# GpSimd's differences, memsets and low parts in pieces, and a later start of the first down weight sums, in a transformer block in float16 parts

## The chip, the cores and the metric

The kernel runs on one core of a Trainium2 chip. The core has four computing engines: TensorE (PE, matrix products into PSUM), VectorE (DVE), ScalarE (ACT) and GpSimd (POOL). SyncE (SP) issues most of the DMAs. Each engine works through a queue of its own in order, and the engines wait for one another by semaphores. The metric is device time in microseconds (us) of one execution. "PEld" in the profile is PE's loading of stationary operands.

## What is computed

One pre-norm transformer block on 2048 tokens of width 640: attention with 32 heads of width 20, in which a query sees the 256 positions up to its own, and a gated feed-forward with 1536 inner columns.

```python
x = A_x                                    # 1 x 2048 x 640, float32
h = x + A(layernorm(x), wqkv, wo)          # sliding window, W = 256
h2 = h + (gelu(n @ w_gate) * (n @ w_up)) @ w_down      # n = layernorm(h)
```

## The kernel before

**Numbers.** A float32 matrix is scaled by a power of two and split into two float16 parts, high (`xh`, `w5h`) and low (`xl`, `w5l`). The high part is a cast on ACT. The low part is the scaled value less the high part, made on POOL or DVE. A product is then three float16 products.

**Order.** The program is written out once, by a planner in Python (`Clock` and the loop at the end of `block_kernel`): lanes (generators) yield an engine and a condition, a modelled clock says when an engine would be free and an operand ready, and the lane that may go issues its next instruction. What is printed is one fixed queue for each engine. `Engine.cost` holds the planner's durations. A lane's condition (`when=`) sets when the planner may issue an instruction; the chip knows only the semaphore waits that follow from the data.

**The head.** `big_lane` fills constant rows of the keys' ring `kT` with memsets on POOL, as soon as q's weights have a scale. `x_cast` makes the parts of the first two blocks of x: ACT's cast `xh`, then POOL's difference `xl`. Beside it DVE makes the low parts of k's weights (`w1l`), and DVE's `qks` takes q's products out of PSUM, so that PE's next product finds a free bank. PE fills its waits there with products of an identity (`pv<-ident`), which stand in its queue.

**The feed-forward.** It runs over four chunks of 512 tokens and three groups of 512 inner columns, each in four tiles of 128. For most of them the gate and up products are made in a scheme of seven block products instead of eight (`Quad`; Strassen's scheme as Winograd wrote it). It needs sums of weight blocks (`weight_sums`: tile `ws`, four parts: POOL makes the third, DVE the first and second, POOL the fourth, two buffers) and sums of token blocks (`token_sums`, on DVE, tiles `ts` and `wst`). The sums are made for the first twelve quads, written to DRAM and read back for the later ones. In a quad PE's results in the PSUM banks `ra`, `rb` and `tp` are copied by ACT (`rr`, `gelt`, `rs`) and summed by DVE (`gel`, `rs`).

**The down product** of the last groups uses the same scheme (`down7`). Its weight sums (`seven_weights`) are four parts of the tile `ts0`: POOL makes t1 from the low parts `w10l`, DVE t2, POOL t3, DVE t4. Its token sums (`seven_tokens`) lie in the space of `w9l`. `seven_weights` may begin, in the planner, when four quads are through.

**Normalisation.** `norm_lane` normalises the next chunk's blocks two at a time beside the quads (lanes h and i): DVE's statistics, POOL's power `lyh`, `lyi`, DVE's small steps on `lyi`, DVE's scaling `wsl`, ACT's cast of it, and transposes by DMA.

All instructions carry one line in the profile, L199, that of the planner's call; groups are told apart by their tiles.

## Time and profile before

| | before |
|---|---|
| median of 3 runs | 996.2 us (995.93 to 996.38) |
| profiled execution | 996.4 us, of which the span is 994.7 |
| PE busy | 977.8 us |
| DVE busy | 787.4 us |
| ACT busy | 485.7 us |
| POOL busy | 342.0 us, 498 instructions |
| HBM read, written | 73.73 MB, 28.84 MB |

The span runs from the first to the last instruction; 1.7 us of the execution lie around it. The mean granted clock of PE is 0.996. By stages: up to some 150 us the inputs are loaded and split and attention starts; attention runs to some 560 us; from some 640 us the quads run, with the down products between them; from 800 us all down products but the last use the scheme of seven. The profile's timeline has start, duration, engine, operation and tiles, and in brackets the idle time of that engine just before, with what ended it.

### The profile page before, as it was taken

To read this page: it belongs to the slowest core of one execution; us is meant where nothing else is said; L and a number is where in the kernel's file an instruction comes from. 1 tells how busy PE (TensorE), PEld (TensorE's weight loads), DVE (VectorE), ACT (ScalarE), POOL (GpSimd) and SP (SyncE) were. 2 spreads that over 40 slices of the span, in tenths; PEclk is the share of its full clock that TensorE was granted. 3 is DMA by queue.
4 is the path that set the end of the run, shared out by engine and by line. 5 is a ranking of instruction groups with operands and counts; after the bars stand their busy time and mean duration, and the time that the engine had idled before them with its cause. 6 is when DMAs were issued, how large, how long until landed. Compare 5 with 4: busy or idle time off the path is not lost.

```text
span 994.7 us, 35811 instructions
## 1 busy us (share of the span) xinstructions
PE 977.8 (98%) x15326; PEld 747.6 (75%) x15326; DVE 787.4 (79%) x2252; ACT 485.7 (49%) x862; POOL 342.0 (34%) x498
## 2 busy tenths in 40 slices
PE   8998999999999999999999999999999999999998
PEld 7875777777877777777766754688788888888886
DVE  7878998887876767777688798877976887788784
ACT  5615657675555555555577535343323333443431
POOL 7003335463434333344346311344303223233320
PEclk9999999999999999999999999999999999999999
DMA  8667565752522433222305543324354442223211
GB/s 314 126 124 181 148 171 161 172 140 76 112 81 70 109 87 81 72 69 70 124 31 124 113 136 104 109 80 132 119 175 106 148 144 81 80 80 107 81 54 53
DMA packets 130047, 113.01 MB, mean 114 GB/s; under 512 B 85216, under 2 KB 103392, under 8 KB 129888
## 3 DMA queue, kind: packets, MB, share of 16 engines
q1 hardware_dynamic: 117792, 99.97, 36.6%
q10 hardware_dynamic: 12096, 10.75, 3.4%
q8 instruction: 120, 1.97, 0.8%
q14 instruction: 39, 0.32, 0.1%
HBM read 73.73 MB, written 28.84 MB: 103 GB/s over the span
## 4 chain that ended last, share of the span: by engine, by line
PE 86%; DVE 8%; ACT 3%; DMA 2%; issue 1%; POOL 0%; SPq 0%; ACTq 0%; DVEq 0%
PE mm L199 40%; PE rb L199 12%; PE ra L199 12%; PE pv L199 11%; PE tp L199 9%; DVE junk L199 1%; DVE ts L199 1%; DVE am L199 1%; ACT pt L199 1%; DVE ht L199 1%; DMA wst<-in_wu_dram 0%; DVE w1l L199 0%; DMA wst<-in_wd_dram 0%; DMA pt<-in_x_dram 0%; DVE xt L199 0%
## 5 line engine op out<-in xcount | busy, mean ns | idle before, releaser
L199 POOL TENSOR_SCALAR_AFFINE_SELECT pt<-pt 128x512 f32<-128x512 f32 x352 | 176.5, 517 | 270.0 <-ACT pt L199 252.6
L199 DVE CUSTOM_DVE_ANT_0 junk<-rb,band 128x320 bf16<-128x320 f32 x232 | 113.4, 489 | 36.1 <-PE rb L199 31.1
L199 ACT ACTIVATE pt<-ra,esc 128x640 f32<-128x640 f32 (+2 forms) x132 | 100.6, 769 | 78.0 <-PE ra L199 68.8
L199 ACT ACTIVATE pt<-rb,esc 128x640 f32<-128x640 f32 (+2 forms) x124 | 94.3, 768 | 81.9 <-PE rb L199 75.4
L199 DVE CUSTOM_DVE_ANT_0 junk<-ra,band 128x320 bf16<-128x320 f32 x216 | 105.7, 489 | 33.9 <-PE ra L199 28.9
L199 PE MATMUL pv<-pt,v 128*21 128x128 f32 x2880 | 103.0, 275 | 0.3 <-ACT oT L199 0.2
L199 PEld LDWEIGHTS <-ah 128*128 128x128 f16 (+1 forms) x660 | 63.5, 98 | 23.2 <-issue 1.0
L199 PEld LDWEIGHTS <-ws 128*128 128x128 f16 x720 | 70.8, 98 | 12.9 <-issue 2.6
L199 PEld LDWEIGHTS <-qT 60*64 60x64 f16 x1280 | 29.7, 104 | 62.3 <-issue 51.3
L199 PEld LDWEIGHTS pv<-pt,v 128*21 128x21 f32 x2880 | 69.2, 100 | 9.6 <-issue 1.1
L199 PEld LDWEIGHTS <-kT 62*64 62x64 f16 x2880 | 64.4, 106 | 9.3 <-issue 5.3
L199 PEld LDWEIGHTS <-gu 128*128 128x128 f16 (+1 forms) x700 | 51.7, 98 | 26.1 <-issue 0.4
L199 DVE SCALAR_TENSOR_TENSOR ht<-mm,ffk,ht 128x320 f32<-128x320 f32 x86 | 46.9, 545 | 15.4 <-PE mm L199 14.2
L199 PE MATMUL mm<-xh,w1h 128*32 128x256 f16 (+1 forms) x344 | 55.9, 273 | 1.4 <-DVE qks L199 1.4
L199 PE MATMUL mm<-xl,w1h 128*32 128x256 f16 (+1 forms) x362 | 56.0, 273 | 0.0
L199 PE MATMUL mm<-xh,w1l 128*32 128x256 f16 (+1 forms) x356 | 55.9, 273 | 0.0
L199 ACT CAST ah<-gel 128x512 f16<-128x512 f32 x48 | 29.7, 619 | 47.8 <-DVE gel L199 47.7
L199 DVE TENSOR_TENSOR al<-gel,ah 128x512 f16<-128x512 f32 x48 | 42.3, 882 | 13.1 <-ACT ah L199 12.1
L199 ACT ACTIVATE gel<-gel,ffk 128x512 f32<-128x512 f32 x36 | 26.0, 723 | 50.2 <-DVE gel L199 50.1
L199 PE MATMUL mm<-w3h,oh 128*32 128x320 f16 (+1 forms) x364 | 49.7, 299 | 0.6 <-DVE ht L199 0.6
L199 PE MATMUL mm<-w3h,ol 128*32 128x320 f16 (+1 forms) x355 | 49.6, 299 | 0.0
L199 PE MATMUL mm<-w3l,oh 128*32 128x320 f16 (+1 forms) x355 | 49.6, 299 | 0.0
(354 smaller groups left out, 2670.2 us busy)
## 6 DMA issues: line engine op xcount, KB each, us to landing
ws<-wsums SPq DMA_DIRECT2D x24, 640.0 KB
qk<-qks ACTq DMA_DIRECT2D x32, 256.0 KB
wsums<-ws SPq DMA_DIRECT2D x12, 640.0 KB
qT<-qk SPq DMA_DIRECT2D x72, 80.0 KB
kT<-qk SPq DMA_DIRECT2D x72, 80.0 KB
ht<-in_x_dram SPq DMA_DIRECT2D x16, 320.0 KB
h_dram<-ht SPq DMA_DIRECT2D x16, 320.0 KB
ht<-h_dram SPq DMA_DIRECT2D x16, 320.0 KB
```

The costliest lines, as they stand in the source:

```text
L199: r = real(*args, **kw)
```

## The change

A helper `difference` issues a subtraction on POOL as several instructions along the first free dimension. Five kinds of differences go through it: the low parts of x's first two blocks (five columns of 128 as 2, 2 and 1), the third and fourth part of the weight sums (the same cut), the first and third down weight sums (four pieces of 320), and two of the down token sums (two pieces of 256). The memsets of `kT` are cut in four. The down weight sums may begin, in the planner, after ten quads instead of four.

```diff
+    def difference(o, a, b, n):
+        for i in range(0, o.shape[1], n):
+            k = slice(i, min(i + n, o.shape[1]))
+            nc.gpsimd.tensor_tensor(o[:, k], a[:, k], b[:, k], op=ALU.subtract)
...
-                nc.gpsimd.memset(kT[64 * par + 32:64 * par + 64, :, r, :].bitcast(F32), pair)
+                for p in range(0, H // 2, 4):
+                    nc.gpsimd.memset(kT[64 * par + 32:64 * par + 64, p:p + 4, r, :].bitcast(F32),
+                                     pair)
...
-        nc.gpsimd.tensor_tensor(lo, src, hi, op=ALU.subtract)
+        difference(lo, src, hi, 2)
...
-        yield on("gpsimd", when=lambda: pos["quads"] >= FT and W["u", 1].spent
+        yield on("gpsimd", when=lambda: pos["quads"] >= 2 * FT + 2 and W["u", 1].spent
...
-            nc.gpsimd.tensor_tensor(t1, d2, d1, op=ALU.subtract)
+            difference(t1, d2, d1, 1)
...
-            nc.gpsimd.tensor_tensor(t3, t2, d1, op=ALU.subtract)
+            difference(t3, t2, d1, 1)
...
-                nc.gpsimd.tensor_tensor(s2, s1, h1, op=ALU.subtract)
+                difference(s2, s1, h1, 2)
...
-                nc.gpsimd.tensor_tensor(s3, h1, h2, op=ALU.subtract)
+                difference(s3, h1, h2, 2)
...
-        nc.gpsimd.tensor_tensor(t[:, 2], gl, ul, op=ALU.subtract)
+        difference(t[:, 2], gl, ul, 2)
...
-        nc.gpsimd.tensor_tensor(t[:, 3], gh, t[:, 1], op=ALU.subtract)
+        difference(t[:, 3], gh, t[:, 1], 2)
```

The change moves instructions. In the head, POOL's queue (`kT` the keys' ring, `xl` the low parts of the first two blocks, `lyxc` the power of the third block's normalisation) reads so, with - for before and + for the change:

```order
 L199 TENSOR_TENSOR lyxb<-lvexb,mhalf 128x1
-L199 MEMSET kT 32x16x64 x12
-L199 TENSOR_TENSOR xl<-gu,xh 128x5x128 x2
+L199 MEMSET kT 32x4x64 x40
+L199 TENSOR_TENSOR xl<-gu,xh 128x2x128 x2
+L199 TENSOR_TENSOR xl<-gu,xh 128x128
+L199 TENSOR_TENSOR xl<-gu,xh 128x2x128 x2
+L199 TENSOR_TENSOR xl<-gu,xh 128x128
 L199 TENSOR_TENSOR lyxc<-lvexc,mhalf 128x1
+L199 MEMSET kT 32x4x64 x8
```

Eight of the 48 shorter memsets now stand behind `xl` and `lyxc`.

In the quads, about 690 to 750 us, POOL's queue before reads (`ws` weight sums, `lyh` and `lyi` powers of the normalisation, `ts` the down weight sums of w10):

```order
L199 TENSOR_TENSOR ws<-w5l,w8l 128x640
L199 TENSOR_TENSOR ws<-w5h,ws 128x640
L199 TENSOR_TENSOR ts_16367<-w10l 128x1280
L199 TENSOR_TENSOR ts_16367<-ts_16367,w10l 128x1280
L199 TENSOR_TENSOR lyh<-lveh,mhalf 128x1
L199 TENSOR_TENSOR lyi<-lvei,mhalf 128x1
L199 TENSOR_TENSOR ws<-gu 128x640
```

and in the change, from the same pair of weight sums on:

```order
L199 TENSOR_TENSOR ws<-w5l,w8l 128x256 x2
L199 TENSOR_TENSOR ws<-w5l,w8l 128x128
L199 TENSOR_TENSOR ws<-w5h,ws 128x256 x2
L199 TENSOR_TENSOR ws<-w5h,ws 128x128
L199 TENSOR_TENSOR lyh<-lveh,mhalf 128x1
L199 TENSOR_TENSOR lyi<-lvei,mhalf 128x1
L199 TENSOR_TENSOR ts_16903<-w10l 128x320 x4
L199 TENSOR_TENSOR ts_16903<-ts_16903,w10l 128x320 x4
L199 TENSOR_TENSOR ws<-gu 128x256 x2
```

The sums of w10 have gone behind the next pair of powers; the first four pieces wait for no semaphore there, the second four for DVE's sum.

On DVE the two sums that belong to them go some sixty rows back. What now stands there (`rs`, `gel` the quad's sums, `ht` the down product's accumulation):

```order
L199 TENSOR_TENSOR rs<-rb,rs 128x256
L199 TENSOR_TENSOR gel<-rb,rr 128x256
L199 SCALAR_TENSOR_TENSOR ts_16903<-w10h,ts_16903 128x1280
L199 SCALAR_TENSOR_TENSOR ts_16903<-ts_16903,w10h 128x1280
L199 SCALAR_TENSOR_TENSOR ht<-mm,ffk,ht 128x320
L199 TENSOR_TENSOR rs<-ra,gelt 128x256
```

Between `gel` and `ht` there was nothing before; the two stood between accumulations of two quads earlier. PE's and SP's queues hold the same operations in the same order as before; on ACT one activation moves by two rows.

## The prediction

> **What bounds the kernel now.** I read the page's busy shares and its chain first, then the windows, to see where TensorE (PE) has room at all.

> ```profile
> PE 977.8 (98%) x15326; PEld 747.6 (75%) x15326; DVE 787.4 (79%) x2252; ACT 485.7 (49%) x862; POOL 342.0 (34%) x498
> PE 86%; DVE 8%; ACT 3%; DMA 2%; issue 1%; POOL 0%; SPq 0%; ACTq 0%; DVEq 0%
> ...
> 92.00:96.00 4.00, 2.16 (x39) 1.03 (x37) 3.83 (x10) 2.29 (x5) 2.12 (x3) 1.00 0.81 237
> 96.00:100.00 4.00, 3.71 (x31) 2.21 (x35) 3.43 (x16) 2.78 (x5) 1.40 (x1) 0.57 0.54 168
> ...
> 703.00:707.00 4.00, 1.80 (x15) 1.18 (x13) 3.96 (x4) 1.10 (x3) 2.48 (x1) 1.00 0.41 164
> 707.00:711.00 4.00, 4.00 (x22) 2.94 (x22) 4.00 (x7) 1.17 (x4) 0.28 (x1) 0.57 0.44 122
> ...
> 800.00:960.00 160.00, 160.00 (x1372) 133.99 (x1370) 130.42 (x205) 64.27 (x142) 45.34 (x27) 1.00 0.27 94
> ```

> The first two lines are the page, the others windows (from:to, length, then busy time of PE, weight loads, DVE, ACT, POOL, and the granted clock). PE is the path: it is busy 98%, and from 800 to 960 us without a break. GpSimd (POOL) has two thirds of its time free and none of the chain, so its pieces matter only where they hold up VectorE (DVE) or PE. PE's losses are few. The largest lies at 703 to 711 us: 2.20 us idle (4.00 less 1.80), and then a clock of 0.57 over 4 us, which is 0.43 x 4 = 1.72 us of lost clock. At 92 to 100 us the same pair stands: 1.84 us idle, then 0.57.

> The timeline shows who made the larger gap.

> ```profile
> 700.62 0.83 DVE L199 SCALAR_TENSOR_TENSOR ws<-ws,w8h 128x640 f16<-128x640 f16 x1 [0.31 <-POOL ws L199]
> 701.52 1.40 POOL L199 TENSOR_TENSOR ws<-w5h,ws 128x640 f16<-128x640 f16 x1 [0.94 <-DVE lyai L199]
> 701.54 1.39 DVE L199 TENSOR_TENSOR lyi<-lyi,lyai 128x1 f32<-128x1 f32 x1
> 702.41 0.71 PE L199 MATMUL ra<-ts,ws 128*128 128x256 f16 x5
> 702.88 2.60 POOL L199 TENSOR_TENSOR ts<-w10l 128x1280 f16<-128x1280 f16 x1
> 702.97 2.85 DVE L199 TENSOR_SCALAR wsl<-wsl,lmvi,lyi 128x640 f32<-128x640 f32 x1
> 705.90 0.72 ACT L199 CAST wsl<-wsl 128x640 f16<-128x640 f32 x1 [6.59 <-DVE wsl L199]
> 706.53 0.37 ACT L199 COPY rr<-tp 128x256 f32<-128x256 f32 x1
> 706.95 1.03 PE L199 MATMUL tp<-h1l,ws 128*128 128x256 f16 x5 [2.20 <-ACT rr L199]
> ...
> 779.67 1.39 POOL L199 TENSOR_TENSOR ws<-gu,ws 128x640 f16<-128x640 f16 x1 [0.94 <-DVE lyai L199]
> 781.11 0.61 DVE L199 TENSOR_SCALAR wsl<-wsl,lmvi,lyi 128x640 f32<-128x640 f32 x1
> 782.85 0.42 PEld L199 LDWEIGHTS <-ws 128*128 128x128 f16 x4 [0.16 <-issue]
> ```

> DVE's one-element `lyi` takes 1.39 us because POOL's `ws` runs; its scaling `wsl` takes 2.85 us because POOL's `ts` of 2.60 us began just ahead. ACT's cast waits for `wsl`, ACT's copy `rr` stands behind that cast, and PE behind `rr`. The last three rows are a natural control 79 us later: the same normalisation beside the same `ws`, but no `ts` behind it. There `wsl` takes 0.61 us, and PE loses 0.16.

> **The change part by part.** Prices of a piece first, by shape:

> ```profile
> L199 POOL TENSOR_TENSOR ws<-w6h,ws 128x640 f16<-128x640 f16 x4 | 5.6, 1399 | 11.4 <-DVE ws L199 11.4
> L199 POOL TENSOR_TENSOR ts<-w11l 128x1280 f16<-128x1280 f16 x2 | 5.2, 2610 | 20.1 <-PE mm L199 20.1
> L199 POOL MEMSET kT<- 32x1024 f32 x12 | 11.5, 1004 | 0.1
> L199 POOL MEMSET mask<- 128x256 f32 x1 | 0.3, 312 | 0.0
> ```

> From 640 to 1280 elements a difference grows by 1.211 us, so 1.89 ns an element and 0.19 us fixed. Estimates: 256 elements 0.67 us, 128 0.43, 320 0.79. A 640 difference becomes 1.77 instead of 1.40, a 1280 one 3.17 instead of 2.61. All pieces together add some 22 us to an engine that is idle for 650.

> (a) The moved `ts` and the gap at 703. In the order, POOL's `ts` of w10 now stands behind the next `lyh`, `lyi`, so nothing follows `ws` at 702.9. `lyi` waits for one piece of `ws` (0.67 for 1.40), then `wsl` for the next (0.67): 1.34 against 1.40, even. The quad's first `ws`, ahead of DVE's sum at 700.62, ends 0.3 later, three pieces for one, and all behind it with it. So I take the control's 0.16 plus some of the 0.3: a gap of 0.3 us is left, 1.9 us gained (0 left if `wsl` passes ahead of the second piece; 0.9 left if it waits for both).

> (b) The clock. With 0.3 us idle in place of 2.20 I expect no dip: 1.7 us gained (0, if the dip has another cause).

> (c) At 632.73 a DVE sum waits for a `ws` in the same way.

> ```profile
> 632.73 1.63 DVE L199 SCALAR_TENSOR_TENSOR ws<-w9h,w9l 128x640 f16<-128x640 f16 x1
> 634.87 0.30 PE L199 MATMUL mm<-w10h,ah 128*128 128x320 f16 x1 [0.22 <-DVE ht L199]
> ```

> A piece takes at most 0.67, so PE's 0.22 us goes: gain 0.2 (bounds 0 and 0.22). At 782.85 the later `ws` costs what it may cost in (a): loss 0.3 (bounds 0 and 0.6).

> (d) The head. POOL's memsets and `xl` stand beside DVE's low parts `w1l`, which hold up the `qks` that PE waits for.

> ```profile
> 7.45 11.58 POOL L199 MEMSET kT<- 32x1024 f32 x12
> 17.65 1.34 ACT L199 CAST xh<-gu 128x640 f16<-128x640 f32 x2
> 19.11 3.34 POOL L199 TENSOR_TENSOR xl<-gu,xh 128x640 f16<-128x640 f32 x2
> 19.76 1.43 DVE L199 SCALAR_TENSOR_TENSOR w1l<-gu,sw,w1h 128x640 f16<-128x640 f32 x1
> 21.18 1.95 DVE L199 SCALAR_TENSOR_TENSOR w1l<-gu,sw,w1h 128x640 f16<-128x640 f32 x1
> 23.46 1.66 DVE L199 SCALAR_TENSOR_TENSOR w1l<-gu,sw,w1h 128x640 f16<-128x640 f32 x2
> 25.04 0.74 DVE L199 SCALAR_TENSOR_TENSOR qks<-mm,qs,qks 128x512 f16<-128x512 f32 x1
> 25.83 0.27 PE L199 MATMUL mm<-xh,w1h 128*128 128x256 f16 x1 [1.38 <-DVE qks L199]
> ```

> A `w1l` alone takes 0.83 (1.66 for two), so the first two wait 0.60 and 1.12 us: 1.72 in all. A memset of 256 costs between 0.24 (a quarter of 11.58/12) and 0.312 (the mask's row); twelve followed each other at 0.04 less than their duration, so I take 0.27. Forty then end at 18.25 instead of 19.03, and `xl` starts when ACT's first cast is done, near 18.35, 0.76 earlier. It lasts 3.4 instead of 2.8, so 2.0 us of it is left at 19.76. If DVE waits for every piece, it waits about as long as before; where its sums follow each other without a gap, or an operation with one SBUF input comes between, it doesn't: at best 0.9 is won. I take 0.2. If memsets cost 0.312, they end at 19.93; `xl` then alternates with five `w1l` and ends near 20.6 + 3.4 + 4 x 0.83 = 27.3, and PE, which needs it at its second product, loses 1.5 (2.4, if two `w0l` get in between). Two scalings of DVE that run beside the first memsets end sooner, and I cost that at nothing: the copies behind them stand on ACT behind its sums of q's weights; without that cover it would be a gain, of less than one memset, 1.0 us.

> (e) The new place of `ts`. Its rows have no wait there, so POOL starts as soon as `lyi` is done, at 733.35 in times of before, right under the next normalisation.

> ```profile
> 709.16 1.48 DVE L199 SCALAR_TENSOR_TENSOR ts<-w10h,ts 128x1280 f16<-128x1280 f16 x1
> ...
> 732.79 0.56 POOL L199 TENSOR_TENSOR lyi<-lvei,mhalf 128x1 f32<-128x1 f32 x1
> 733.51 0.61 DVE L199 TENSOR_SCALAR wsl<-wsl,lmvh,lyh 128x640 f32<-128x640 f32 x1
> 735.28 0.42 DVE L199 TENSOR_TENSOR rs<-ra,rr 128x256 f32<-128x256 f32 x1
> 737.50 0.71 PE L199 MATMUL ra<-h1h,w6l 128*128 128x256 f16 x5
> 743.15 0.42 DVE L199 TENSOR_TENSOR rs<-ra,gelt 128x256 f32<-128x256 f32 x1
> 746.76 0.71 PE L199 MATMUL ra<-h1h,w6l 128*128 128x256 f16 x5
> ```

> Four pieces of 0.79 alternate with `wsl`, `lyi` and the second `wsl`. Two waits of 0.6 to 0.8 put `rs` 1.4 us later, to 737.1 at its end; PE needs that bank at 737.50. Then DVE's own two sums of `ts`, 1.48 each (the first row, where no POOL work lies beside it), move in ahead of 743.15: with a wait of 0.8 for a piece, `rs` ends near 746.9, and PE wants its bank at 746.76. So the margins are 0.4 and about nothing; I take a loss of 0.4 (bounds 0 and 1.5, by one more piece at each place).

> (f) The other pieces of `ts` and the token sums `w9l`: PE stands still nowhere between 800 and 960, and the products that read them come several us later. Nothing, and without that cover 0.15 to 0.5 us each.

> Sum against the profiled execution (996.4, of which 994.7 is the span): -1.9 -1.7 -0.2 +0.3 -0.2 +0.4 = -3.3, so 993.1. The runs' median is 0.2 lower: **992.9 us**. The end follows, since from 800 us on PE works without a break.

> [...]

> **Rivals.** (1) The dip stays: the half clock follows something else than the idle time, and only the gap goes. For it: the dip starts behind the gap, and I have two cases only. Against: both of the longest gaps have it. -3.3 + 1.7: 994.6. [...]
> (2) The change moves the collision rather than removing it: at (e) PE waits 1.5 us, and where that brings a dip, 1.7 more. For: no wait holds the moved rows. Against: pieces, and no ACT cast behind `wsl` there. 994.0 to 995.7.
> (3) The head: memsets at 0.31, `xl` late, 1.5 to 2.4 lost instead of 0.2 won: 994.6 to 995.5.
> (4) Slower: the weight sums' chain. `ws` on POOL, DVE's sum (ends at 701.45), PE's product at 702.41: 0.96 us of slack, in each of twelve quads. If DVE gets in at every piece boundary (0.83 each) and 0.3 is added, the two boundaries cost 1.96, and PE waits 1.0 in each: 12 us, 1005. It decides from 0.96 us on. Against: between the two DVE sums of a quad stand mostly operations on PSUM.

> **How the numbers follow.** Forecast 0.64, 992.9, in itself 991.5 to 994.0; (1) 0.08; (2) 0.13; (3) 0.09; (4) 0.06. Faster by over 0.2% (below 994.2; 0.2%, 2 us, is about what a measurement tells from no change): 0.64 + 0.03 + 0.03 + 0.02 = 0.72; within: 0.22, the rest of (1) to (3); slower: 0.06, (4). The range takes the forecast's best, with 0.7 more at the head (991.0), and reaches past (1), (2) and (3) to 996.0; outside stay (4) and some 0.1 of unknown sizes.

> **What would show it.** `wsl` at 703 near 1.2 us or less, PE's gap below 0.5, no 0.57 behind it, PE waits near 737 and 746 below 0.5 each, PE's start at 25.83 unchanged within 0.9. Wrong if the windows from 640 to 800 show PE idle in each quad, or a dip at another place.

## The result and the profile after

| | before | after |
|---|---|---|
| median of 5 runs | 996.2 us (995.44 to 996.38) | 991.0 us (990.46 to 991.52) |
| profiled execution | 996.4 us, span 994.7 | 991.5 us, span 989.8 |
| mean granted clock of PE | 0.996 | 0.998 |

The ratio after to before is 0.9949 (95% interval 0.9936 to 0.9962): faster by 5.2 us, where 3.3 were forecast. The page of the changed kernel, its busy times and its chain:

```profile
PE 975.3 (99%) x15326; PEld 746.1 (75%) x15326; DVE 779.5 (79%) x2252; ACT 485.9 (49%) x862; POOL 376.4 (38%) x636
PE 87%; DVE 8%; ACT 3%; DMA 1%; issue 1%; SPq 0%; POOL 0%; ACTq 0%; DVEq 0%
```

POOL is 34.4 us busier (342.0 before) and still has no share of the chain. DVE is 7.9 us less busy with the same 2252 instructions. The largest part is `al<-gel,ah`, 48 subtractions of the same shape, 5.0 us less in sum. I read this as time in which DVE stood, counted as busy, behind POOL: most of these subtractions take 0.69 us, those beside POOL's differences up to 2.77 before and up to 1.29 after. The windows that answer to those of before (busy PE, weight loads, DVE, ACT, POOL, then the granted clock):

```profile
92.00:96.00 4.00, 2.04 (x44) 0.96 (x40) 3.68 (x11) 1.40 (x4) 1.54 (x2) 0.90 0.58 173
96.00:100.00 4.00, 3.81 (x47) 2.62 (x40) 3.57 (x15) 3.62 (x6) 2.08 (x2) 0.68 0.47 157
703.00:707.00 4.00, 4.00 (x38) 3.44 (x36) 3.28 (x7) 2.19 (x6) 0.00 (x0) 1.00 0.69 220
707.00:711.00 4.00, 4.00 (x37) 3.30 (x35) 1.75 (x5) 0.63 (x4) 0.00 (x0) 1.00 0.89 267
```

From 703 to 711 us PE has neither a gap nor a half clock any more. The stall at 92 to 100 us is as it was. The timeline shows why the gap is gone (start, duration, engine, operation):

```profile
700.92 1.93 POOL L199 TENSOR_TENSOR ws<-w5h,ws 128x256 f16<-128x256 f16 x3 [0.94 <-DVE lyai L199]
...
700.94 0.66 DVE L199 TENSOR_TENSOR lyi<-lyi,lyai 128x1 f32<-128x1 f32 x1
701.64 0.93 DVE L199 TENSOR_SCALAR wsl<-wsl,lmvi,lyi 128x640 f32<-128x640 f32 x1
...
702.64 0.73 ACT L199 CAST wsl<-wsl 128x640 f16<-128x640 f32 x1 [4.22 <-DVE wsl L199]
703.27 0.37 ACT L199 COPY rr<-tp 128x256 f32<-128x256 f32 x1
...
703.69 0.71 PE L199 MATMUL tp<-h1l,ws 128*128 128x256 f16 x5
```

`lyi` now takes 0.66 us (1.39 before) and `wsl` 0.93 (2.85). The copy `rr` ends at 703.64, and PE's product starts at 703.69 with no idle time in brackets.

To see where time is won or lost along the program, take the same product of PE in two traces and subtract its starts. Each column below is such a product, named by its time in the kernel before; numbers are us against the profiled execution of before, negative where earlier. The last column is the change from 704.4 to the last product. (In `e4_fill` the 19 added products are left out of the count.)

```
              25.8  172.8  624.9  632.9  644.2  704.4  707.1  711.3  739.5  786.4  last | 704-end
after        -1.04  -0.55  -0.77  -0.36  -0.93  -0.90  -3.26  -4.92  -4.45  -4.57  -4.57 | -3.67
e7_after     -1.53  -1.29  -1.14  -0.73  -1.31  -1.28  -3.65  -5.31  -5.31  -5.43  -5.44 | -4.16
e1_head      -1.15  -0.64  -0.86  -0.86  -0.86  -0.87  -0.82  -0.89  -0.89  -0.90  -0.74 | +0.13
e2_late      -0.19  -0.10  -0.21  -0.22  -0.22  -0.23  -2.47  -4.14  -3.53  -2.73  -2.73 | -2.50
e3_pieces    +0.02  +0.03  +0.04  +0.45  -0.13  -0.06  -2.42  -4.09  -4.09  -4.21  -4.21 | -4.15
e4_fill      +0.08  +0.72  +1.61  +1.60  +1.60  +1.60  +1.60  -0.07  -0.07  -0.07  -0.07 | -1.67
e5_no_late   -0.98  -0.45  -0.57  -0.16  -0.74  -0.71  -3.08  -4.74  -4.74  -4.86  -4.86 | -4.15
e6_w3l       -1.02  -0.38  -0.47  -0.06  -0.64  -0.61  -2.98  -4.64  -4.64  -4.76  -4.76 | -4.15
e8_memset    -0.26  +0.29  +0.51  +0.51  +0.51  +0.50  +0.56  +0.39  +0.39  +0.38  +0.38 | -0.12
e9_xl        -0.98  -1.09  -0.82  -0.81  -0.82  -0.81  -0.81  -2.48  -2.48  -2.48  -2.48 | -1.67
e10_ts_head  -1.24  -0.95  +0.39  +0.39  +0.38  +0.38  -1.44  -3.11  -3.11  -3.11  -3.11 | -3.49
e11_again    -1.20  +2.13  +2.12  +2.53  +1.95  +1.97  -0.40  -2.06  -2.06  -2.18  -2.18 | -4.15
e12_ws_head  -1.19  -0.88  -1.03  -0.62  -1.20  -1.15  -3.52  -5.18  -3.96  -4.08  -4.08 | -2.93
```

In the row `after` one reads: the head brings 1.04, half of it is given back by 172.8; the gap at 703 brings 2.36, the clock behind it 1.66, a wait near 733 costs 0.47, and two small steps bring 0.16 (632 to 644) and 0.12 (at 782). Up to 644 us the executions of one kernel differ by half a microsecond and more (`after` and `e7_after` are the same kernel; `e11_again`, the kernel of `e11_w3l_again`, lost 3 us ahead of 172.8). From 704 us on they repeat better: four executions with all three kinds of sums cut and the early start give -4.15 each. The two of the changed kernel still differ there by 0.49 (-3.67 and -4.16), for a reason that comes below. So the last column is the sharper measure, and medians carry the rest.

### The profile page after: what moved, and what is told of

Read it like the earlier page. It is cut to its first block, busy times and chain, and to the rows that moved or that the text cites. A ratio compares the mean times of both kernels' runs of the same rounds, so it can differ in the third digit from the quotient of the medians.

```text
span 989.8 us, 35966 instructions
## 1 busy us (share of the span) xinstructions
PE 975.3 (99%) x15326; PEld 746.1 (75%) x15326; DVE 779.5 (79%) x2252; ACT 485.9 (49%) x862; POOL 376.4 (38%) x636
## 3 DMA queue, kind: packets, MB, share of 16 engines
q8 instruction: 120, 1.97, 0.8%
## 4 chain that ended last, share of the span: by engine, by line
PE 87%; DVE 8%; ACT 3%; DMA 1%; issue 1%; SPq 0%; POOL 0%; ACTq 0%; DVEq 0%
PE mm L199 41%; PE rb L199 13%; PE ra L199 12%; PE pv L199 11%; PE tp L199 9%; DVE junk L199 1%; DVE ts L199 1%; DVE am L199 1%; ACT pt L199 1%; DMA qT<-in_wqkv_dram 1%; DVE ht L199 0%; DVE w1l L199 0%; DVE gel L199 0%; DVE al L199 0%; DMA kT<-qk 0%
## 5 line engine op out<-in xcount | busy, mean ns | idle before, releaser
L199 POOL TENSOR_SCALAR_AFFINE_SELECT pt<-pt 128x512 f32<-128x512 f32 x352 | 176.4, 517 | 270.3 <-ACT pt L199 252.8
L199 DVE CUSTOM_DVE_ANT_0 junk<-rb,band 128x320 bf16<-128x320 f32 x232 | 113.4, 489 | 36.2 <-PE rb L199 31.3
L199 ACT ACTIVATE pt<-ra,esc 128x640 f32<-128x640 f32 (+2 forms) x132 | 100.6, 769 | 78.0 <-PE ra L199 69.7
L199 ACT ACTIVATE pt<-rb,esc 128x640 f32<-128x640 f32 (+2 forms) x124 | 94.3, 768 | 81.9 <-PE rb L199 77.7
L199 DVE CUSTOM_DVE_ANT_0 junk<-ra,band 128x320 bf16<-128x320 f32 x216 | 105.7, 489 | 33.9 <-PE ra L199 28.9
L199 PE MATMUL pv<-pt,v 128*21 128x128 f32 x2880 | 102.8, 275 | 0.3 <-ACT oT L199 0.2
L199 PEld LDWEIGHTS <-ah 128*128 128x128 f16 (+1 forms) x660 | 63.5, 98 | 23.0 <-issue 0.8
L199 PEld LDWEIGHTS <-ws 128*128 128x128 f16 x720 | 70.4, 98 | 10.1
L199 PEld LDWEIGHTS <-qT 60*64 60x64 f16 x1280 | 29.7, 104 | 62.3 <-issue 51.3
L199 PEld LDWEIGHTS pv<-pt,v 128*21 128x21 f32 x2880 | 69.1, 100 | 9.6 <-issue 1.1
L199 PEld LDWEIGHTS <-kT 62*64 62x64 f16 x2880 | 64.4, 106 | 9.7 <-issue 5.8
L199 PEld LDWEIGHTS <-gu 128*128 128x128 f16 (+1 forms) x700 | 51.6, 98 | 26.1 <-issue 0.3
L199 DVE SCALAR_TENSOR_TENSOR ht<-mm,ffk,ht 128x320 f32<-128x320 f32 x86 | 46.8, 545 | 14.8 <-PE mm L199 13.6
L199 PE MATMUL mm<-xh,w1h 128*32 128x256 f16 (+1 forms) x344 | 55.9, 273 | 0.5 <-DVE qks L199 0.5
L199 PE MATMUL mm<-xl,w1h 128*32 128x256 f16 (+1 forms) x362 | 56.0, 273 | 0.0
L199 PE MATMUL mm<-xh,w1l 128*32 128x256 f16 (+1 forms) x356 | 55.9, 273 | 0.0
L199 ACT CAST ah<-gel 128x512 f16<-128x512 f32 x48 | 29.7, 619 | 43.3 <-DVE gel L199 43.2
L199 PE MATMUL mm<-w3h,oh 128*32 128x320 f16 (+1 forms) x364 | 49.7, 299 | 0.6 <-DVE ht L199 0.6
L199 PE MATMUL mm<-w3h,ol 128*32 128x320 f16 (+1 forms) x355 | 49.6, 299 | 0.0
L199 PE MATMUL mm<-w3l,oh 128*32 128x320 f16 (+1 forms) x355 | 49.6, 299 | 0.0
L199 PE MATMUL mm<-xl,w0h 128*32 128x256 f16 (+1 forms) x361 | 49.4, 273 | 0.0
L199 PE MATMUL mm<-xh,w0l 128*32 128x256 f16 (+1 forms) x361 | 49.4, 273 | 0.0
```

Of the source, the lines that this page charges most:

```text
L199: r = real(*args, **kw)
```

## The experiments

**First set: which part does what.** Times against 995.9 us for the kernel before on the same chip. One experiment does the head alone:

```diff
+                for p in range(0, H // 2, 4):
+                    nc.gpsimd.memset(kT[64 * par + 32:64 * par + 64, p:p + 4, r, :].bitcast(F32),
+                                     pair)
...
-        nc.gpsimd.tensor_tensor(lo, src, hi, op=ALU.subtract)
+        difference(lo, src, hi, 2)
```

> Only the head's two edits (memsets of kT in four, low parts of x's first two blocks in pieces); everything from 640 us on as before. Theory: the head's gain is its own, PE's first product of k starts near 24.9 (25.83 before), a load near 170 us takes part of it back, the gap of 2.20 us at 703 and the half clock behind it stay. 995.4 to 995.8, that is 0.4 to 0.8 less than before. Rival: the head's gain is all lost again by the loads, 996.2; or none is lost, 995.2.

Measured: 995.7 us, ratio 0.9993 (0.9984 to 1.0002). PE's product started at 24.68, the gap of 2.20 us at 703 stayed. By the table 1.15 us are won at 25.8 and 0.64 are left at 172.8. The mechanism came as expected; the median, 0.2 us lower, can't tell the head's gain from nothing. It isn't taken at equal clock either: 9 of these 11 runs had a mean clock of 0.997 or less, and 13 of the 32 of the kernel before. Among the runs with that clock the means are 995.7 and 997.4 us, so the median may well hide a gain; how large it is stays open.

The next does the later start alone, with whole differences:

```diff
-        yield on("gpsimd", when=lambda: pos["quads"] >= FT and W["u", 1].spent
+        yield on("gpsimd", when=lambda: pos["quads"] >= 2 * FT + 2 and W["u", 1].spent
```

> Only the later start of the down weight sums, all differences whole. Theory: PE's gap at 703 falls to 0.2 to 0.5 us and no half clock follows, but at the new place the whole ts of 2.6 us stands under the normalisation's lyh, lyai and wsl, so that rs comes later and PE waits 1.5 to 3 us near 733, with a half clock behind it where the wait is near 2 us: 994 to 996.5. Rival: at the new place there is slack for a whole ts, the later start alone is the gain: 992.2 to 992.8.

Measured: 994.49 us, ratio 0.9987 (0.9978 to 0.9996). The stall at 703 and the half clock are gone (-3.91 from 704.4 to 711.3), and 1.41 us come back at the new place. The timeline there:

```profile
729.18 2.63 POOL L199 TENSOR_TENSOR ts<-w10l 128x1280 f16<-128x1280 f16 x1
...
729.24 2.58 DVE L199 SCALAR_TENSOR_TENSOR lyai<-lyi,lvei 128x1 f32<-128x1 f32 x1
731.74 0.60 DVE L199 TENSOR_SCALAR wsl<-wsl,lmvh,lyh 128x640 f32<-128x640 f32 x1
...
733.50 0.42 DVE L199 TENSOR_TENSOR rs<-ra,rr 128x256 f32<-128x256 f32 x1
...
733.97 0.71 PE L199 MATMUL ra<-h1h,w6l 128*128 128x256 f16 x5 [0.45 <-DVE rs L199]
...
748.94 0.71 PE L199 MATMUL ra<-h1h,w9h 128*128 128x256 f16 x5 [0.64 <-ACT rs L199]
```

A DVE step of one element stands for 2.58 us behind the whole `ts`; `rs` comes late, and PE waits. The 1.41 us are a little less than the 1.5 to 3 expected. This is the rival "the change moves the collision", real for a whole `ts`, though no half clock followed.

The third does the pieces of the three kinds of sums alone (the third and fourth part of `ws`, the first and third of `ts`, two token sums; a line of each):

```diff
+        difference(t[:, 2], gl, ul, 2)
...
+            difference(t1, d2, d1, 1)
...
+                difference(s2, s1, h1, 2)
```

> Only the pieces of the weight sums, the down weight sums and the token sums; their start and the head as before. Theory: wsl at 703 waits for one or two pieces of 0.8 us, not for 2.6; PE's gap falls to 0.9 or less and no half clock follows: 992.7 to 993.6. Rival: VectorE gets in only once GpSimd has issued all four pieces, so the gap stays near 2 us and the half clock too: 995.8 to 996.4.

Measured: 992.8 us, ratio 0.9969 (0.9956 to 0.9981). -4.15 from 704.4 to the end, without the later start. So two edits of the change each remove the same stall at 703, and their gains don't add.

The fourth asks what the clock follows. It is the kernel before with products on PE whose result nobody reads:

```diff
             yield self.then("m5", self.y, self.s[:, 3], self.l2)
+            if self.i == 6:
+                idle = psum.tile([P, 512], F32, name="pv", tag="pv", bufs=1)
+                for _ in range(19):
+                    tc.nc.tensor.matmul(idle[:, :CW], self.gh[:, 0], self.h2[:, 0], start=True,
+                                        stop=True)
```

> The kernel before, with 19 more products of 128x256 on PE (some 2.07 us, result unused) ahead of the product that waits 2.20 us at 703. The wait of the useful work stays, PE is busy in it. Theory: the half clock follows PE's idle time, so it is gone: 1.6 to 1.7 us less than before, 994.5, mean granted clock 0.998. Rival: the half clock follows something else (the throttle by load, a fixed phase): 0.57 stays in the 4 us behind it, 996.2 to 996.4, mean clock 0.996.

Measured: 995.85 us, ratio 0.9995 (0.9986 to 1.0003), mean clock 0.998 in the profiled execution. The windows of this kernel, and below them the ones of the kernel before at its half clock:

```profile
703.00:707.00 4.00, 4.00 (x36) 3.30 (x35) 3.93 (x4) 0.00 (x0) 3.88 (x2) 1.00 0.43 169
707.00:711.00 4.00, 3.87 (x36) 3.30 (x35) 3.96 (x8) 2.33 (x6) 0.08 (x1) 1.00 0.22 41
```

```profile
703.78:707.19 3.41, 1.21 (x11) 0.79 (x9) 3.37 (x4) 1.27 (x3) 1.70 (x1) 1.00 0.46 185
707.19:710.61 3.42, 3.42 (x19) 2.42 (x17) 3.42 (x6) 0.99 (x2) 0.00 (x0) 0.50 0.40 101
```

With PE busy the useful product waits as long as before (2.21 us, from 706.34 to 708.55) and the half clock doesn't come: -1.67 from 704.4 on, the whole price of the dip, as the theory had it. The total hides it, since this execution came 1.6 us late to 704.4, where the edit has done nothing yet. The median of the 11 runs doesn't show it either. On the total alone the theory would have failed; the segment decides. One rival has to be shut out, since `e9_xl` (last section) has the same gap without a half clock, because a border of the windows described there cuts it in two, 1.19 and 1.01 us. Here, counted from the half clock at 97.711 us, a window runs from 705.28 to 708.70: the whole wait lies inside one, so it isn't the border that spared it.

**Second set: is the later start needed, and is there more to win?** Times against 995.96 us. The first kernel is the change without the edit of the later start, and beside it runs the changed kernel itself:

```diff
-        yield on("gpsimd", when=lambda: pos["quads"] >= 2 * FT + 2 and W["u", 1].spent
+        yield on("gpsimd", when=lambda: pos["quads"] >= FT and W["u", 1].spent
```

> All pieces of the change, but the down weight sums start where they did before. Theory: either of the two edits alone takes the stall at 703 away, and the later start only adds the wait near 733 (0.32 us in the changed kernel), so here PE waits 0.15 us or less at 703 and not at all from 730 to 755; 0.3 to 0.5 us less than the changed kernel on the same chip. Rival: the pieces at the old place leave a wait of 0.3 to 0.5 at 703 and the two kernels are even.

> The changed kernel itself, as the reference for the others on this chip: 4.5 to 5.3 us less than before.

Measured: 991.24 us, ratio 0.9959 (0.9945 to 0.9972), and for the changed kernel 991.59 us, 0.9964 (0.9951 to 0.9978), 4.4 us less than before where 4.5 to 5.3 were expected. In the former PE is busy from 700 to 755 us without a break:

```profile
700.00:755.00 55.00, 55.00 (x472) 45.95 (x471) 43.10 (x94) 16.86 (x38) 18.43 (x23) 1.00 0.45 135
```

But the changed kernel's wait near 733, 0.32 us in the first profile, was absent in its second one (-5.31 through 739.5), so the two are even within what was measured. The wait goes with a race of two instructions; the two profiles of the same changed kernel, first and second:

```profile
728.38 0.81 DVE L199 TENSOR_TENSOR lyh<-lyh,lyah 128x1 f32<-128x1 f32 x1
728.39 3.28 POOL L199 TENSOR_TENSOR ts<-w10l 128x320 f16<-128x320 f16 x4
...
729.11 0.82 DVE L199 SCALAR_TENSOR_TENSOR lyai<-lyi,lvei 128x1 f32<-128x1 f32 x1
729.86 1.16 DVE L199 TENSOR_SCALAR wsl<-wsl,lmvh,lyh 128x640 f32<-128x640 f32 x1
...
733.05 0.71 PE L199 MATMUL ra<-h1h,w6l 128*128 128x256 f16 x5 [0.32 <-DVE rs L199]
```

```profile
727.98 0.16 DVE L199 TENSOR_TENSOR lyh<-lyh,lyah 128x1 f32<-128x1 f32 x1
727.99 3.30 POOL L199 TENSOR_TENSOR ts<-w10l 128x320 f16<-128x320 f16 x4
...
728.06 0.76 DVE L199 SCALAR_TENSOR_TENSOR lyai<-lyi,lvei 128x1 f32<-128x1 f32 x1
728.74 1.16 DVE L199 TENSOR_SCALAR wsl<-wsl,lmvh,lyh 128x640 f32<-128x640 f32 x1
```

Both engines start within about 0.01 us of each other, DVE first in both. Where `lyh` loses, DVE waits for one piece more, 0.65 us (0.81 against 0.16), and PE sees 0.32 of it.

The next kernel goes after the stall that was left at 92 to 100 us, where DVE's `lyx` waits for a whole `w3l` (the output weights' low part) on POOL:

```diff
-                nc.gpsimd.tensor_tensor(lo, w, hi, op=ALU.subtract)
+                if self.col == C_WO:
+                    for k in (slice(0, 256), slice(256, 512), slice(512, 640)):
+                        tc.nc.gpsimd.tensor_tensor(lo[:, k], w[:, k], hi[:, k], op=ALU.subtract)
...
```

> The kernel of e5_no_late with the output weights' low parts (w3l) cut into 256, 256 and 128 as well, at the same places in every queue. Theory: VectorE's lyx near 92 us falls from 1.22 to 0.7 or less and PE's wait of 1.96 us at 95 to 1.2 to 1.5; but what is won there is gone by 173 us, because a load of the gate weights that ends near 170 us doesn't come earlier: within 0.2 us of e5_no_late. Rival: 0.5 to 1.1 us of it is kept to the end.

> The kernel of e6_w3l once more, since its lead over e5_no_late (990.47 against 991.24) is smaller than the runs spread. Theory: nothing of the 0.4 us won at 95 us is left at 173, so its median lies within 0.3 us of e12_ws_head's, if that is like e5_no_late. Rival: it is 0.5 to 1 us less.

Measured: 990.47 us, ratio 0.9948 (0.9936 to 0.9961), and again 991.32 us, 0.9952 (0.9938 to 0.9966) against 996.42. PE's wait at 95 us fell only to 1.53 us (1.93 in `e5_no_late`), short of the 1.2 to 1.5 expected, and at 172.8 the profile stands 0.07 us behind that of `e5_no_late`. In the second execution PE waited at that place for 3.02 us, for a load of keys and not for DVE. Both had also waited for a load of keys at 53 us (0.45 and 1.00 us), so the profiles can't settle it. All these intervals overlap with that of the changed kernel: a version that beats it isn't shown, and what cutting `w3l` is worth stays open.

The last of this set has the head's memsets alone, and its partner from the third set the pieces of `xl` alone:

> Only the memsets of kT in four, all else as before. Theory: VectorE's two scalings beside the first memsets end up to 0.4 us earlier and the memsets 0.6 us earlier, but whole low parts xl still hold w1l up: PE's first product of k at 25.5 to 25.8 us (25.83 before, 24.7 with both edits). Rival: the memsets give all of it, 24.7 to 24.9.

> Only the low parts of x's first two blocks in pieces, memsets whole. Theory: the memsets alone moved PE's first product of k to 25.57 us, the rest of the head's gain is w1l passing between pieces of xl: 24.9 to 25.2 us here. Rival: the pieces of xl help only behind the shorter memsets: 25.5 to 25.9.

Measured, one run each: 996.46 and 993.61 us, PE's product at 25.57 and 24.85 us. Since the loads ahead of it shift by 0.5 us between executions, the interval from DVE's maximum of k's weights (`am<-ra`, 17.29 us in the kernel before) to that product is better:

```
memsets, xl whole   (before, e2, e3, e4)          8.54  8.82  8.73  8.82
memsets cut         (e8)                          8.30
xl in pieces        (e9)                          8.20
both                (after, e7, e5, e1, e12, e10) 7.66  7.67  7.66  7.78  7.66  7.66
```

From a mean of 8.73 the memsets bring 0.43, the pieces of `xl` 0.53, both 1.05. Neither rival holds: within the 0.28 us by which the first row spreads, the two add up.

**Third set: which pieces.** Times against 996.42 us. In these two only the weight sums, or only the down weight sums, are cut; both have the head's edits and the early start. The first two lines are the one's, the last two the other's:

```diff
+        difference(t[:, 2], gl, ul, 2)
...
+        difference(t[:, 3], gh, t[:, 1], 2)
...
+            difference(t1, d2, d1, 1)
...
+            difference(t3, t2, d1, 1)
```

> The head's pieces and the weight sums' (ws) pieces alone; the down weight sums and token sums are whole and start where they did before. Theory, from the rows of e5_no_late, where wsl ran from 701.81 to 702.74, between two pieces of ws and before the first ts: it is the pieces of ws that let wsl pass, so a whole ts behind them holds nothing up at 703: PE waits 0.2 us or less there, no half clock, within 0.3 us of e5_no_late (991.0 to 991.5). Rival: the pieces of ts do it; here wsl waits for the whole ts, PE 1.5 to 2.2 us, and the time is 993 to 995.

> The head's pieces and those of the down weight sums (ts) alone; weight sums and token sums are whole, starts as before. Theory: lyi waits for a whole ws (1.4 us), so ts is under way when wsl comes, and wsl waits for one piece of 0.8: PE waits 0.5 to 0.9 us at 703 in place of 2.20, no half clock: 0.5 to 1 us more than e5_no_late. Rival: the pieces of ts alone do as well as all (0.2 us or less), or don't help (2 us).

Measured: 992.68 us, ratio 0.9966 (0.9954 to 0.9979), and 992.71 us, 0.9959 (0.9945 to 0.9973). With `ws` cut, PE has no gap at 703, as the theory said; but it isn't like `e5_no_late`, since 1.22 us come back by 739.5. Timeline of the kernel with `ws` cut:

```profile
709.01 2.61 POOL L199 TENSOR_TENSOR ts<-ts,w10l 128x1280 f16<-128x1280 f16 x1 [3.86 <-DVE ts L199]
...
709.19 3.78 DVE L199 SCALAR_TENSOR_TENSOR ts<-ts,w10h 128x1280 f16<-128x1280 f16 x1
712.89 0.41 DVE L199 TENSOR_TENSOR rs<-rb,rs 128x256 f32<-128x256 f32 x1
...
715.01 0.71 PE L199 MATMUL ra<-h1h,w6l 128*128 128x256 f16 x5 [1.06 <-DVE rs L199]
```

This is a second stall that lay hidden behind the first. DVE's sum of `ts` stands 2.3 us behind POOL's whole second `ts`, `rs` and what follows come late, and PE, no longer late itself, waits. In the kernel before the same sum took 3.78 us too, and PE did not wait for it:

```profile
710.89 3.78 DVE L199 SCALAR_TENSOR_TENSOR ts<-ts,w10h 128x1280 f16<-128x1280 f16 x1
```

With `ts` cut it takes 1.97 (`e5_no_late`, at 709.27), and PE doesn't wait.

With `ts` cut and `ws` whole, PE waits 0.39 us at 703 (0.5 to 0.9 expected), with no half clock, and nothing comes back later (-3.49 from 704.4 on, 0.66 less than `e5_no_late`, where 0.5 to 1 was expected): `lyi` takes 1.39 us as before, and `wsl` 1.04. So each kind of pieces has its own work at this place, and the later start does the work of both, except that it needs the pieces of `ts` at its new place.

## Why the prediction was right, step by step

Direction, place and mechanism of the two largest terms were right. The size was less so: 991.0 is at the very end of the range, 1.9 us below the forecast and below the 991.5 to 994.0 that the forecast gave itself. It is inside only because the range had room for 0.7 more at the head. Of the 1.6 us that the span gained beyond the forecast the head kept 0.35; (a) and (c) brought 0.46 and 0.38, and some 0.5 came from stretches to which no term belonged. That all this just fitted is luck. The terms, forecast against the profiled execution (by the table, `after`):

| step | forecast | came |
|---|---|---|
| (a) gap at 703 | -1.9 | -2.36 |
| (b) clock behind it | -1.7 | -1.66 |
| (c) 632 to 644 / 782 | -0.2 / +0.3 | -0.16 / -0.12 |
| (d) head, at 25.8 / kept at 172.8 | -0.2 | -1.04 / -0.55 |
| 172.8 to 624.9 | none | -0.22 |
| (e) new place of `ts` | +0.4 | +0.47 (0 in the second profile) |
| (f) other pieces | 0 | 0 |
| 644.2 to 704.4 | none | +0.03 |
| behind the last product | none | -0.3 |
| span | -3.3 | -4.9 |

**(a)** The mechanism was right: the collision of `wsl` with `ts` is gone, no new one took its place, and the other bound came (0 left). Its condition did not: `wsl` doesn't pass ahead of the second piece but waits for the rest of it (0.93 us against 0.61 alone), and is early enough all the same. What I didn't see is that the pieces alone, at the old place, do it too (`e3_pieces`, `e5_no_late`), and that a hidden second stall of about 1 us at 715 had to go as well for the gain to last (`e12_ws_head`).

**(b)** Right in size and in cause: `e4_fill` took the dip away by keeping PE busy. The rival that it follows something else has fallen. The condition is finer than the length of a gap (the same 2.20 us brought none in `e9_xl`), and in part of the executions there is no dip to win back (last section). That the kernel before's profiled execution had it was chance.

**(c)** At 782.85 the step "one piece, then the next, 1.34 against 1.40, even" failed. `lyi` and `wsl` together took 1.59 us (0.66 and 0.93, at 775.52 and 776.22) where they had taken 2.00. I had charged DVE a whole piece at each step, but DVE comes when a piece is partly done, and waits for its rest. That POOL's first `ws` of the quad would end 0.3 later held: DVE waits 0.59 for it, 0.31 before.

```profile
774.60 0.82 DVE L199 SCALAR_TENSOR_TENSOR ws<-ws,gu 128x640 f16<-128x640 f16 x1 [0.59 <-POOL ws L199]
```

At 632.73 DVE's `ws` fell from 1.63 to 1.01 us, but PE's wait moved ahead of it: the pieces get between DVE's three `w9l` (2.49 us for 2.08), `gel` comes later, and PE waits 0.60 us there instead of 0.19 and 0.22. It is paid back by 640 us; the sum was right, the step was not.

```profile
629.30 2.49 DVE L199 SCALAR_TENSOR_TENSOR w9l<-wst,sw,w9h 128x512 f16<-128x512 f32 x3 [3.10 <-ACT w9h L199]
...
632.37 1.01 DVE L199 SCALAR_TENSOR_TENSOR ws<-w9h,w9l 128x640 f16<-128x640 f16 x1
632.50 0.30 PE L199 MATMUL mm<-w10h,ah 128*128 128x320 f16 x1 [0.60 <-DVE gel L199]
```

**(d)** This was the mis-sized term. It rested on "if DVE waits for every piece, it waits about as long as before". The rows of after:

```profile
18.70 5.67 POOL L199 TENSOR_TENSOR xl<-gu,xh 128x256 f16<-128x256 f32 x6 [0.57 <-ACT xh L199]
...
19.61 1.07 DVE L199 SCALAR_TENSOR_TENSOR w1l<-gu,sw,w1h 128x640 f16<-128x640 f32 x1
20.67 0.98 DVE L199 SCALAR_TENSOR_TENSOR w1l<-gu,sw,w1h 128x640 f16<-128x640 f32 x1
21.98 2.10 DVE L199 SCALAR_TENSOR_TENSOR w1l<-gu,sw,w1h 128x640 f16<-128x640 f32 x2
24.00 0.74 DVE L199 SCALAR_TENSOR_TENSOR qks<-mm,qs,qks 128x512 f16<-128x512 f32 x1
24.80 0.27 PE L199 MATMUL mm<-xh,w1h 128*128 128x256 f16 x1 [0.49 <-DVE qks L199]
```

Against 0.83 alone the four `w1l` wait 0.24, 0.15 and 0.44 us, 0.83 in all, where they waited 1.72. The other condition of that sentence, an operation with one SBUF input in between, holds for some operations only. In the trace of before the statistics `lsth` take 0.48 us beside POOL's differences as without them, and `ht` and `rs`, with an input in PSUM, 0.54 and 0.42 beside them, 0.55 and 0.42 without; the scaling `wsl`, of one wide input in SBUF, takes 2.85 beside `ts` and 0.61 alone. `qks` comes 1.04 earlier and so does PE. POOL pays: `xl` lasts 5.67 us rather than 3.34, and since PE needs it only later, nobody waits. (The 3.4 us taken for these six pieces was itself low: by the prediction's own prices, two times 1.77, they take 3.5.) The memsets came out at the 0.27 that I took (13.0 us for 48, in the rows under (f)). Of the 1.04, 0.49 are given back by 172.8; in this trace PE's wait there follows ACT, which had waited 0.52 us for a load of the gate weights:

```profile
169.94 0.72 ACT L199 ACTIVATE gu<-wsl,sw 128x512 f16<-128x512 f32 x1 [0.52 <-DMA wsl<-in_wg_dram]
...
172.21 0.34 PE L199 MATMUL ra<-qT,kT 62*64 62x128 f16 x12 [0.35 <-ACT pt L199]
```

That the loads are what takes it back is read from the profile; no experiment moved them, and other executions kept more (1.09 in `e9_xl`).

**(e)** Right in sum: a loss of 0.47 at the first of the two places, none at the second; the margin of 0.4 is decided by one piece. At the second the margin was about 0.5 and not nothing (`rs` ends at 741.81, PE's product starts at 742.31), since DVE's second sum of `ts` took 1.49 us and waited for no piece. `e2_late` shows what (e) would have cost without pieces: 0.6 us at the first place, and 0.8 not at the second but at a product some 5 us behind it (748.94 in its trace).

**(f)** Right: PE works without a break from 800 to 955 us.

```profile
800.00:955.00 155.00, 155.00 (x1330) 129.82 (x1328) 123.91 (x198) 61.93 (x138) 60.73 (x69) 1.00 0.28 94
```

POOL's extra busy time is 34 us rather than 22, because its pieces wait for DVE in turn. A piece of 128 behind which nothing of DVE lies takes 0.43 us as estimated, one beside the normalisation 0.60. The groups of after by line and shape (count, then busy us, mean ns):

```profile
L199 POOL MEMSET kT<- 32x256 f32 x48 | 13.0, 320 | 0.2
...
L199 POOL TENSOR_TENSOR ws<-w5h,ws 128x128 f16<-128x128 f16 x4 | 2.4, 604 | 0.0
...
L199 POOL TENSOR_TENSOR ws<-w6h,ws 128x128 f16<-128x128 f16 x4 | 1.7, 430 | 0.0
```

**The rivals.** (1) fell with `e4_fill`. (2) came in a small form (0.32 us, or nothing). (3) fell: the memsets take 0.27, and PE starts earlier. (4), the slower case, fell: between the products of 644.2 and 704.4, through six quads, the change loses 0.03 us, so PE felt nothing of what the weight sums' chain lost in slack.

## What to carry to other kernels

A long operation on GpSimd can hold up even a one-element step of VectorE (2.58 us beside a `ts` of 2.63 in `e2_late`); where GpSimd has time to spare, as here (busy 342.0 of 994.7 us), cutting it into pieces trades idle GpSimd time for VectorE's waits (34.4 us more busy time on GpSimd, 7.9 less on VectorE), and the place to look first is a short VectorE step with an ACT copy and a PE bank behind it. When a stall goes, look in the same trace for the operation that was already long but hidden behind it. And measure small edits by the distance between the same two products in two traces: here the runs of one kernel spread by 1 to 5 us, while one stretch repeated to 0.01 in four executions where no race stood in it. Before a theory on the clock is dropped or kept for a median, see how many runs of each kernel had the half clock.

## What the runs showed of the hardware

```
half clock in the next window: idle 1.88 1.90 1.95 1.95 1.95 1.95 2.00 2.03 2.19 2.20 2.30 2.39 3.02
no half clock:                 idle 0.90 0.98 1.00 1.17 1.19 1.28 1.44 1.49 1.55
```

From 20 us to the last products no other window has a half clock behind it, the most idle of them with 1.66 us (`e4_fill`, at 22.6). So the limit in these traces lies between 1.66 and 1.88 us of idle time inside one window, and where the grid lies differs from one execution to the next (half clocks start at 96.205 us in the kernel before and at 95.179 in `after`). `e9_xl` has the same gap of 2.20 us at 703 as the kernel before, and no dip; a border cuts the gap in two, 1.19 and 1.01 us:

```profile
701.72:705.13 3.41, 2.22 (x18) 1.55 (x16) 3.37 (x3) 0.04 (x1) 2.94 (x2) 1.00 0.48 192
705.13:708.54 3.41, 2.40 (x23) 2.15 (x23) 3.37 (x7) 2.25 (x6) 0.00 (x0) 1.00 0.25 48
708.54:711.95 3.41, 3.41 (x31) 2.83 (x29) 3.41 (x3) 1.07 (x2) 2.04 (x1) 1.00 0.68 179
```

The gap's 1.66 us of clock are thus not a fixed price but one that is paid in part of the executions: 22 of 54 runs of the kernel before had a mean clock of 0.997 or less (two dips, to judge by the profiled executions: 0.996 in the kernel before with two, 0.998 in `after` with one), and 7 of 66 runs of the kernels in which the idle time at 703 is gone or below 0.4 us. A window without any work of PE wasn't needed for a dip: 1.88 of 3.41 us of idle time were enough (`e5_no_late`, the window from 93.738).

**The dip at 96 us cost 0.33 us by 103, the one at 707 cost 1.66.** At 96 us the half clock was absent in `e2_late` and `e3_pieces`, which put PE 1.06 us ahead by 99.7 (same product, against the kernel before). At 101 us nothing of that was left and at 103 us 0.33 in each: PE waited instead, 0.49 us for DVE's maxima and 0.37 for DVE's `o` (`e3_pieces`, at 99.66 and 100.45).

**DVE and POOL took turns at the borders of instructions.** In the rows of after at 701 us `lyi` ends with POOL's first piece of `ws`, `wsl` gets in behind the second, and the third, of 128, takes 0.68 us where one alone takes 0.43: the DVE operation that waited went next at the border, and POOL's next piece waited for it. How many pieces DVE waited for hung on less than 0.01 us at the start near 728 us: there `lyh` starts 0.007 us ahead of POOL's first piece in the one profile and 0.011 in the other, and it waits in the first alone. Beside a whole instruction of POOL the wait lasted to its end: in `e2_late` DVE's step of one element, begun 0.06 us behind `ts`, took 2.58 us, and `ts` 2.63. In `after` `lyi` waited for one piece and took 0.66 us, where beside the whole `ws` it had taken 1.39; that is why pieces help here.
